# The first routing of an attention and mixture-of-experts chain: where its ranks, late parts, exponentials and first transposes stand in the order

## The chip, the cores and the metric

The program runs on one core of one Trainium2 chip. The metric is the device time of one execution in microseconds (us), as the median of several runs; for the kernel before it is 500.62 us (three runs, 499.69 to 501.07).

## The reference

Three stages follow each other. A linear attention with a decaying state runs over two sequences of 768 tokens (8 heads of 48). Its output, as 1536 tokens of 384 numbers, goes through a mixture of 8 experts where each token takes one (with a capacity of 384), and the result through a second one where each token takes two of 8, with noise in its gate.

```
state = alpha[t, :, None] * state + k[t] (x) v[t];   y[t] = q[t] . state        # per head
x = y as (1536, 384)
logits = x @ w_gate;  e = argmax;  gate = softmax(logits)[e]                    # layer 1
out1[i] = gate[i] * (relu(x[i] @ w1[e]) @ w2[e])     if fewer than 384 tokens came to e before i
noisy = out1 @ w_gate2 + log1p(exp(out1 @ w_noise)) * noise                     # layer 2
top2 of noisy, softmax over the two;  out[i] = sum_k weight[i, k] * (relu(out1[i] @ w1'[e_k]) @ w2'[e_k])
```

## The kernel before

All engines run lists that are written out in program order (`manual_schedule`); each engine takes its own list strictly in order, and a tile framework adds the semaphore waits that the data and the reuse of buffers ask for. PSUM tiles come in three rings: `ph` (3), `py` (3) and `pm` (2).

**Attention.** The tokens are cut into 12 chunks of 128 (6 of each sequence). A letter string says what is issued for chunk i, and in what order: S is `scores` of chunk i+1 (PE transposes the keys and forms two score tiles, ACT copies all three out of PSUM, POOL masks the scores with `affine_select`, L299), T is `state`, L is `logits` of chunk i-1, M is `mix` (the output `y`, copied by ACT as `yT`, L346), D is one step of `decays` (scans and products on VectorE, called DVE here, that prepare keys and queries of the next pieces), W is one split of a first-expert weight into a rounded part (ACT, L523) and a rest (POOL or DVE, L524), and R is one step of the routing. Chunks 0 to 7 use `PATTERN`, chunks 8 to 11 `PATTERN2` (L50 to L52, quoted in the diff).

**Logits.** `r1_logits` (L360) multiplies `yT` with the identity and the gate weights into one `pm` tile. From it DVE sums the gate logits (`gates`, L368), and ACT copies the token rows to SBUF (L389). For the chunks 8 to 11 (`EARLY` = 8) there are also "late parts": a rounded copy of the rows (ACT, L377) and its rest (DVE, `low`, L381), both read from the PSUM tile, since these tokens do not go to the first expert by way of DRAM.

**Routing.** `route1` is a generator for a group of chunks (`GROUPS`, L38: chunks 0 to 2, 3 to 5, 6 and 7, 8 and 9, 10, 11; called groups 0 to 5 here). Its steps are: maximum of the logits; its index; one-hot `oh`; the ranks on PE (L416 to L420, running counts by matrix products with a triangle) together with the exponential on ACT (L422); sums, the product with the rank tile and the reciprocal; slots and counts (L436 to L441); the scatter of the rows to DRAM by indirect DMAs from POOL (L158). Group 2's last step also loads the first expert's early tokens back (L447).

**First expert's tokens.** `first_x` (L589) transposes the early tokens with PE (L595), adds the late tokens by products of late parts with a slot matrix (L602), and splits the sum (ACT L609, DVE L610).

**Experts.** Sixteen jobs (8 experts, two layers) follow. `hidden` (L615) forms one block of 128 hidden units out of nine products, with weights and tokens each split in two parts (L623); `second` (L632) is the second product (L650). `split_x` (L570) transposes and splits the next job's tokens.

## Time and profile before

| what | value |
|---|---|
| median of three runs | 500.62 us (499.69 to 501.07) |
| the profiled execution | 503.19 us, of which the span of the trace is 501.4 us |
| PE (TensorE products) busy | 478.2 us, 95% of the span |
| DVE / ACT / POOL busy | 310.1 / 262.0 / 316.5 us |
| attention and first routing | until 98.51 us, when the first `hidden` starts |

The page gives the busy time of each engine, the span in 40 slices, the chain of work that ended last, and the costliest groups of instructions. PEclk is the TensorE clock granted in a stretch, as a share of 2.4 GHz. Times in the text are us from the start of the span.

### The profile page before, as it was taken

The page shows a single profiled execution, that of the slowest core. Times are in us where ns is not written, and L with a number is a line of the kernel's source. Part 1 is how long each engine was busy: PE and PEld are TensorE (multiplying, and loading weights), DVE is VectorE, ACT ScalarE, POOL GpSimd, SP SyncE. Part 2 cuts the span into 40 slices and gives each one's busy share as a digit, 9 for nine tenths or more (in the row PEclk, how much of TensorE's full clock was granted, in tenths as well). Part 3 has the DMA queues.
Part 4 walks back from the last instruction along what each step waited for, and adds up shares of the span by engine and source line. Part 5 has one row for each costly group of instructions (what it writes and reads, how often), then busy time and mean ns, then how long its engine had stood idle before and what let it go on. Part 6 is the DMA issues. An engine that isn't in the chain of part 4 may idle for free.

```text
span 501.4 us, 9823 instructions
## 1 busy us (share of the span) xinstructions
PE 478.2 (95%) x3539; PEld 448.2 (89%) x3542; DVE 310.1 (62%) x866; ACT 262.0 (52%) x682; POOL 316.5 (63%) x396
## 2 busy tenths in 40 slices
PE   8997999899999999999999799999999999999993
PEld 4586887799999999999988699899999999999993
DVE  8999956656786786776863323925545373655540
ACT  3475686366675676675661248353554535364410
POOL 3444674374876786785864149697594958779322
PEclk9999998999999999999999899999999999999997
DMA  8974663497888777676734644393564927372132
GB/s 287 406 246 160 242 221 127 164 295 233 282 288 249 261 241 241 202 244 203 239 100 130 204 92 132 99 245 106 156 176 129 221 81 203 83 191 25 17 47 43
DMA packets 47798, 91.67 MB, mean 183 GB/s; under 512 B 4624, under 2 KB 29153, under 8 KB 47738
## 3 DMA queue, kind: packets, MB, share of 16 engines
q1 hardware_dynamic: 38090, 70.32, 42.9%
q0 software_dynamic: 9648, 20.61, 17.4%
q8 instruction: 30, 0.49, 0.4%
q14 instruction: 30, 0.25, 0.2%
HBM read 70.63 MB, written 20.28 MB: 181 GB/s over the span
## 4 chain that ended last, share of the span: by engine, by line
PE 73%; DVE 14%; issue 4%; ACT 4%; DMA 2%; POOL 1%; SPq 0%; POOLq 0%; DVEq 0%; ACTq 0%
PE py L650 28%; PE ph L623 27%; DVE s L524 2%; PE pm L582 2%; PE ph L290 2%; DVE h L627 2%; PE pm L366 2%; DVE s L237 2%; PE pm L834 1%; PE py L337 1%; PE pm L678 1%; PE py L343 1%; PE ph L861 1%; ACT s L523 1%; PE py L317 1%
## 5 line engine op out<-in xcount | busy, mean ns | idle before, releaser
L524 POOL TENSOR_TENSOR s<-s,s 128x384 fp32r<-128x384 f32 x175 | 184.8, 1301 | 51.0 <-ACT s L523 45.9
L623 PE MATMUL ph<-x,s 128*128 128x240 f32 (+6 forms) x1152 | 179.9, 311 | 3.1 <-DVE h L627 1.4
L623 PEld LDWEIGHTS ph<-x,s 128*128 128x128 f32 x1152 | 167.6, 189 | 6.9 <-DVE h L627 3.0
L650 PE MATMUL py<-h,s 128*128 128x240 f32 (+5 forms) x1008 | 154.1, 307 | 0.0
L650 PEld LDWEIGHTS py<-h,s 128*128 128x128 f32 x1008 | 142.5, 189 | 1.0
L523 ACT ACTIVATE s<-s 128x384 fp32r<-128x384 f32 x256 | 123.1, 516 | 0.0
L627 DVE SCALAR_TENSOR_TENSOR h<-ph,h 128x240 fp32r<-128x240 f32 (+6 forms) x128 | 61.0, 483 | 67.4 <-ACT h L626 62.0
L524 DVE TENSOR_TENSOR s<-s,s 128x384 fp32r<-128x384 f32 x81 | 89.8, 1128 | 5.6 <-ACT s L523 5.5
L626 ACT ACTIVATE h<-ph 128x240 fp32r<-128x240 f32 (+6 forms) x128 | 55.3, 432 | 62.8 <-PE ph L623 53.5
L158 POOL DMA_INDIRECT out<-b,m_ix x29 | 46.5, 1605 | 45.5 <-ACT b L802 21.0
L586 ACT ACTIVATE x<-pm 128x480 fp32r<-128x480 f32 (+7 forms) x38 | 18.5, 489 | 63.9 <-PE pm L582 63.5
L299 POOL TENSOR_SCALAR_AFFINE_SELECT h<-h 128x512 f32<-128x512 f32 x24 | 22.6, 964 | 39.2 <-ACT h L298 39.2
L158 POOL DMA_INDIRECT xs<-b,m_si x32 | 32.9, 1028 | 15.8 <-DVE pm L759 10.5
L587 DVE TENSOR_TENSOR x<-pm,x 128x480 fp32r<-128x480 f32 (+7 forms) x38 | 20.7, 550 | 31.8 <-ACT x L586 31.5
L650 PE MATMUL py<-s,h 128*128 128x384 f32 x144 | 26.6, 340 | 0.0
L650 PEld LDWEIGHTS py<-s,h 128*128 128x128 f32 x144 | 25.0, 188 | 0.0
L237 DVE TENSOR_TENSOR s<-s,s 112x256 f32<-112x256 f32 (+2 forms) x24 | 19.0, 813 | 0.8 <-DMA s<-qs 0.2
L158 POOL DMA_INDIRECT xs<-s,m_si x12 | 13.1, 1088 | 9.8 <-DVE m_g L405 4.6
L156 POOL MEMSET spacer<- 1x1 f32 x74 | 18.8, 253 | 0.1
L582 PE MATMUL pm<-iw,b 108*128 108x108 f32 (+5 forms) x129 | 18.5, 259 | 0.2 <-DVE accs L760 0.2
L170 PE MATMUL ph<-warm 128*128 128x512 bf16 x63 | 16.2, 410 | 1.7 <-POOL warm L165 1.5
L797 DVE TENSOR_REDUCE m_own<-m_ox 108x4 f32<-108x24 f32 (+1 forms) x6 | 1.1, 176 | 24.6 <-POOL m_ox L795 23.5
(234 smaller groups left out, 544.9 us busy)
## 6 DMA issues: line engine op xcount, KB each, us to landing
s<-w SPq DMA_DIRECT2D x64, 768.0 KB, 5.4
xs<-s SPq DMA_DIRECT2D x2, 1576.0 KB, 6.4
out<-s SPq DMA_DIRECT2D x4, 768.0 KB, 7.8
b<-xs POOLq DMA_DIRECT2D x4, 664.9 KB
b<-xs POOLq DMA_DIRECT2D x7, 369.4 KB
s<-as SPq DMA_DIRECT2D x2, 780.5 KB
s<-ks SPq DMA_DIRECT2D x2, 768.0 KB, 9.5
s<-qs SPq DMA_DIRECT2D x2, 768.0 KB
```

Of the source, the lines that this page charges most:

```text
L156: G.memset(spacer, 0.0)
L158: st = G.indirect_dma_start(out=dst, out_offset=bass.IndirectOffsetOnAxis(ap=ix, axis=0), in_=src, in_offset=None, **kw)
L237: eng.tensor_tensor(o, src[:, h].rearrange("r (s j) -> r s j", j=64), x[:, h].rearrange("r (s j) -> r s j", j=64), op=ALU.mult)
L299: G.affine_select(a_, a_, pattern=[[0, 4], [1, 128]], compare_op=ALU.is_ge, fill=0.0, base=0, channel_multiplier=-1)
L523: A.activation(hi[sl], t[sl], AF.Copy)
L524: rest.append(lambda: (eng or V).tensor_tensor(lo[sl], t[sl], hi[sl].bitcast(F32), op=ALU.subtract))
L582: PE.transpose(xp[:, k * c + sl.start:k * c + sl.stop], g[:r, t, d * 128:(d + 1) * 128], ident[:r, :r])
L587: V.tensor_tensor(m(xl), xp[:, :w], m(xh).bitcast(F32), op=ALU.subtract)
L623: PE.matmul(p, w, x[:, d, :], start=(k == 0), stop=(k == 3 * ND - 1))
L626: A.activation(hh, p, AF.Relu)
L627: V.scalar_tensor_tensor(hl, p, 0.0, hh.bitcast(F32), op0=ALU.max, op1=ALU.subtract)
L650: PE.matmul(out_, l, r, start=(f == 0 and k == 0), stop=(f == NF - 1 and k == 2))
```

## The change

There are five edits.

- Each chunk has its own letter string (`PATTERNS`). The ranks of groups 0 and 1 now come two chunks behind their one-hots, right behind the scores of a later chunk. The weight splits start with three instead of five in chunk 7 and end in chunk 10 as before.
- In `route1` the exponential is a step of its own, ahead of the ranks. Groups take as many steps as before.
- In `r1_logits` the rows are copied out of PSUM first; a late part's rounded copy (ACT) and its rest (now on POOL) are made from that copy in SBUF. For groups of several chunks the gate sums follow the row copies, for single ones they stand ahead of them.
- At the end, `first_x`'s transposes and the ranks of group 4 stand ahead of the logits of chunk 11.
- `hidden` takes the three products with the tokens' low part last.

```
-FX = 4
-FXR = (3, 3, 0, 0)
+FXR = (4, 0, 1, 2)
-PATTERN = "WSDDWTWLRRRDDWMW"
-PATTERN2 = "WSRRRWTRWLRRRWMW"
-PLATE = 8
+PATTERNS = (
+    "SDDTDDM", "SDDTLDDM", "SDDTLDDM", "SDDTLRRRDDM", "SDDTLDDM", "SRRDDTLRRRDDM",
+    "SDDTLRRRDDM", "WSDDTWLDDMW", "WSRRWTRRRWLRRRWMW", "RWSRWTRRRWLWMW", "WSTWLRRRWMW", "RRRRLRRRRM")
...
-            if j >= EARLY:
+            if len(js) == 1:
                 gates()
             by = lambda x: x.rearrange("p (g a e) -> p g a e", g=4, a=2)
+            for ab in range(2):
+                A.activation(by(row[:, k, :DM])[:, :, ab, :], lv[:, :, ab * 64:ab * 64 + 48], AF.Copy)
+            if len(js) > 1:
+                gates()
             if j >= EARLY and first:
                 t = late[j] = sb([128, 2 * DM + C1], "b6", 5, F32R)
-                for ab in range(2):
-                    A.activation(by(t[:, :DM])[:, :, ab, :], lv[:, :, ab * 64:ab * 64 + 48], AF.Copy)
-
-                def low():
-                    for ab in range(2):
-                        V.tensor_tensor(by(t[:, DM:2 * DM])[:, :, ab, :], lv[:, :, ab * 64:ab * 64 + 48],
-                                        by(t[:, :DM].bitcast(F32))[:, :, ab, :], op=ALU.subtract)
-
-                if len(js) > 1:
-                    low()
-                else:
-                    lows.append(low)
-            for ab in range(2):
-                A.activation(by(row[:, k, :DM])[:, :, ab, :], lv[:, :, ab * 64:ab * 64 + 48], AF.Copy)
-            if j < EARLY:
-                gates()
+                A.activation(t[:, :DM], row[:, k, :DM], AF.Copy)
+                G.tensor_tensor(t[:, DM:2 * DM], row[:, k, :DM], t[:, :DM].bitcast(F32), op=ALU.subtract)
...
             V.tensor_tensor(oh, io8[:, None, :].to_broadcast(sh), i8[:, :n, 0:1].to_broadcast(sh), op=ALU.is_equal)
             yield
+            A.activation(ex, lm, AF.Exp)
+            yield
             rp = pm()
...
-            A.activation(ex, lm, AF.Exp)
-            while lows:
-                lows.pop(0)()
...
-                for (w, x) in ((wh, xh), (wh, xl), (wl, xh)):
-                    PE.matmul(p, w, x[:, d, :], start=(k == 0), stop=(k == 3 * ND - 1))
+                for (w, x) in ((wh, xh), (wl, xh)):
+                    PE.matmul(p, w, x[:, d, :], start=(k == 0), stop=False)
                     k += 1
+            for d in range(ND):
+                PE.matmul(p, w1_of(n, f, d)[0], xl[:, d, :], start=False, stop=(d == ND - 1))
...
-        while routes:
-            route_on()
-        logits(NCK - 1)
         fx = first_x()
-        for k in range(FX):
+        for k in FXR:
             next(fx)
-            for _ in range(FXR[k]):
+            for _ in range(k):
                 route_on()
+            if len(groups[-1]) and NCK - 1 not in grp:
+                logits(NCK - 1)
+                for _ in range(5):
+                    route_on()
```

How the order moves, at three places. Names: `pm_...`, `py_...` and `ph_...` are PSUM tiles, `m_oh_576` is the one-hot of group 0, `b_...` are early tokens or late parts.

PE in chunk 4, before: from the logits of chunk 3 to the start of the mix of chunk 4.

```order
L366 MATMUL pm_642<-s_4_80,h_599 128x120 x4
L416 LDWEIGHTS ones
L416 MATMUL pm_650<-eb_183,ones 128x24
L417 LDWEIGHTS ones
L417 MATMUL pm_650<-acc_187,ones 128x24
L419 LDWEIGHTS ones
L419 MATMUL pm_650<-m_oh_576,ones 128x16
L419 LDWEIGHTS ones
L419 MATMUL pm_650<-m_oh_576,ones 128x8
L420 LDWEIGHTS tri
L420 MATMUL pm_650<-m_oh_576,tri 128x24
L337 MATMUL py_666<-s_65_390,s_4_80 112x128 x4
```

PE in chunk 5, now: the same ranks, from the last score product of chunk 6 to the logits of chunk 4.

```order
L289 MATMUL ph_681<-s_81_472,s_80_471 128x128
L406 LDWEIGHTS ones
L406 MATMUL pm_697<-eb_183,ones 128x24
L407 LDWEIGHTS ones
L407 MATMUL pm_697<-acc_187,ones 128x24
L409 LDWEIGHTS ones
L409 MATMUL pm_697<-m_oh_576,ones 128x16
L409 LDWEIGHTS ones
L409 MATMUL pm_697<-m_oh_576,ones 128x8
L410 LDWEIGHTS tri
L410 MATMUL pm_697<-m_oh_576,tri 128x24
L365 MATMUL pm_712<-s_4_80,h_663 128x120 x4
```

The ranks left the place ahead of the mix of chunk 4; the mix of chunk 4 and the scores of chunk 6 now stand ahead of them.

ACT in chunks 9 and 10, before: from a weight split over the late part and the row of chunk 8 to `yT` of chunk 9 (L346).

```order
L523 ACTIVATE s_204_1077<-s_135_757 128x384
L377 ACTIVATE b_209_1089<-pm_1083 128x4x48 x2
L389 ACTIVATE s_206_1080<-pm_1083 128x4x48 x2
L523 ACTIVATE s_204_1077<-s_135_757 128x384
L346 ACTIVATE h_1111<-py_1098 112x512
```

The same stretch of ACT now (`yT` of chunk 9 is L345).

```order
L508 ACTIVATE s_192_1016<-s_168_906 128x384 x2
L374 ACTIVATE s_204_1074<-pm_1077 128x4x48 x2
L379 ACTIVATE b_207_1085<-s_204_1074 128x384
L508 ACTIVATE s_192_1016<-s_168_906 128x384
L345 ACTIVATE h_1103<-py_1090 112x512
```

The row copy came ahead of the late part, which now reads the row and not the PSUM tile.

PE at the end of the attention, before: from the last mix product over the ranks of group 4 to the first late part.

```order
L343 MATMUL py_1238<-h_1137,x_687 48x128
L416 LDWEIGHTS ones
L416 MATMUL pm_1254<-eb_183,ones 128x8
L417 LDWEIGHTS ones
L417 MATMUL pm_1254<-acc_187,ones 128x8
L420 LDWEIGHTS tri
L420 MATMUL pm_1254<-m_oh_1233,tri 128x8
L366 MATMUL pm_1276<-s_4_80,h_1251 128x120 x4
L595 MATMUL py_1287<-iw_83,b_203_1074 128x120 x4
L595 MATMUL py_1288<-iw_83,b_203_1074 128x120 x2
L602 MATMUL py_1287<-b_209_1089 128x240 x4
```

The same stretch of PE now.

```order
L342 MATMUL py_1235<-h_1131,x_671 48x128
L580 MATMUL py_1250<-iw_83,b_203_1070 128x120 x4
L580 MATMUL py_1251<-iw_83,b_203_1070 128x120 x2
L406 LDWEIGHTS ones
L406 MATMUL pm_1259<-eb_183,ones 128x8
L407 LDWEIGHTS ones
L407 MATMUL pm_1259<-acc_187,ones 128x8
L410 LDWEIGHTS tri
L410 MATMUL pm_1259<-m_oh_1229,tri 128x8
L365 MATMUL pm_1276<-s_4_80,h_1248 128x120 x4
L587 MATMUL py_1250<-b_207_1085 128x240 x4
```

The transposes of the early tokens (L595, now L580) moved from behind the logits of chunk 11 to ahead of the ranks and those logits.

## Rows read from the trace of the kernel before

**Rows 1.** The page: the clock granted to TensorE in 40 slices, in tenths.
```profile
PEclk9999998999999999999999899999999999999997
```

**Rows 2.** Busy time by stretch: us, then each engine's busy us, PEclk, DMA share.
```profile
48.00:53.00 5.00, 5.00 (x44) 4.15 (x43) 4.88 (x11) 1.14 (x2) 0.00 (x0) 0.66 0.96 342
...
83.00:87.00 4.00, 3.93 (x22) 3.68 (x24) 2.72 (x15) 3.29 (x10) 1.25 (x3) 0.57 0.58 169
```

**Rows 3.** Timeline of PE, chunks 4 to 8: start, us, work, [idle before <-releaser].
```profile
46.87 0.17 PE L416 MATMUL pm<-eb,ones 1*128 1x24 bf16 x1 [2.40 <-DVE m_l L368]
...
47.70 0.19 PE L419 MATMUL pm<-m_oh,ones 128*128 128x16 bf16 x2 [0.55 <-DVE m_oh L411]
...
47.78 1.11 PE L337 MATMUL py<-s,s 112*112 112x128 f32 x8
...
50.38 1.01 PE L284 MATMUL py<-iw,s 112*128 112x112 f32 x4
...
64.69 1.11 PE L337 MATMUL py<-s,s 112*112 112x128 f32 x8
...
66.74 0.60 PE L284 MATMUL py<-iw,s 112*128 112x112 f32 x4
...
68.36 0.54 PE L315 MATMUL py<-s,iw 48*64 48x192 f32 x4
```

**Rows 4.** Timeline of DVE in the same chunks.
```profile
43.82 2.51 DVE L237 TENSOR_TENSOR s<-s,s 112x768 f32<-112x768 f32 x2
...
47.47 0.18 DVE L411 TENSOR_TENSOR m_oh<-io,m_j 128x24 bf16<-128x24 f32 x1
...
48.86 0.17 DVE L240 COPY s<-s 112x12 f32<-112x12 f32 x1
...
53.38 0.96 DVE L237 TENSOR_TENSOR s<-s,s 112x768 f32<-112x768 f32 x1
...
59.28 2.26 DVE L237 TENSOR_TENSOR s<-s,s 112x768 f32<-112x768 f32 x2
```

**Rows 5.** Timeline of POOL in the same chunks: mask pairs, and the first scatter.
```profile
36.98 2.97 POOL L299 TENSOR_SCALAR_AFFINE_SELECT h<-h 128x512 f32<-128x512 f32 x2 [4.17 <-ACT h L298]
...
55.64 1.20 POOL L158 DMA_INDIRECT xs<-s,m_si  x1
...
60.03 2.00 POOL L299 TENSOR_SCALAR_AFFINE_SELECT h<-h 128x512 f32<-128x512 f32 x2
...
63.39 1.23 POOL L299 TENSOR_SCALAR_AFFINE_SELECT h<-h 128x512 f32<-128x512 f32 x2 [1.35 <-ACT h L298]
```

**Rows 6.** Timeline of ACT at the logits of chunk 8.
```profile
80.27 0.55 ACT L377 ACTIVATE b<-pm 128x192 fp32r<-128x192 f32 x2 [2.39 <-DVE m_l L368]
81.56 0.55 ACT L389 ACTIVATE s<-pm 128x192 f32<-128x192 f32 x2 [0.75 <-DVE b L381]
...
82.42 0.60 ACT L346 ACTIVATE h<-py 112x512 f32<-112x512 f32 x1
```

**Rows 7.** Timeline of PE, chunks 10 and 11 and the first expert's start.
```profile
83.07 1.85 PE L366 MATMUL pm<-s,h 112*128 112x120 f32 x8 [1.24 <-ACT h L346]
...
92.29 1.15 PE L366 MATMUL pm<-s,h 112*128 112x120 f32 x8 [0.52 <-DVE b L381]
93.28 1.50 PE L595 MATMUL py<-iw,b 120*128 120x120 f32 x12
94.54 0.92 PE L602 MATMUL py<-b 128*128 128x240 f32 x6
...
97.25 1.02 PE L602 MATMUL py<-b 128*128 128x240 f32 x6
98.51 1.67 PE L623 MATMUL ph<-x,s 128*128 128x240 f32 x5 [0.23 <-ACT x L609]
```

**Rows 8.** The DMA queue of SP: the load of the early tokens.
```profile
83.57 0.41 SPq L447 DMA_DIRECT2D b<-xs  x1
```

**Rows 9.** Timeline of PE in the tenth job.
```profile
323.25 1.25 PE L623 MATMUL ph<-x,s 128*128 128x432 f32 x5 [1.07 <-DVE x L587]
```

More of the change, by code (lines that the diff above doesn't have):

```diff
@@ L347, in mix @@
             yTs[i] = yT
-        scat1, grp, late, early, lows = [], {}, {}, [], []
+        scat1, grp, late, early = [], {}, {}, []
         def r1_group(js):
@@ L447, in route1 @@
                 nc.sync.dma_start(early[0], xs1[:C1].rearrange("(t p) d -> p t d", p=P1))
-            yield
         parts, raws, rest = {}, {}, []
@@ L988, in body @@
             left_ = int(DECAYS[i])
-            for o in PATTERN if i < PLATE else PATTERN2:
+            for o in PATTERNS[i]:
                 if o == "S" and si < NCK:
```

## The prediction, made before the change was run

> **What bounds the kernel now.** I read the page first. PE is busy for nearly the whole span, and its clock stands at full speed but for two slices with a digit 8 and the last one [rows 1], so the time is PE's own work plus the places where PE waits or runs slowly. The change touches the stage up to 98.51, where the first expert starts, and the order of products inside `hidden`. So next I read PE's timeline of that stage for its bracketed waits, then the windows for the clock behind them, then the timelines of the engines that PE waited for.
>
> Three places lose time. In chunk 4 PE has done the logits of chunk 3 and stands before the ranks of group 0: 2.40 us and then 0.55 us idle [rows 3]. DVE still works off the decays; the two last products of the piece run from 43.82 to 46.33, and the one-hot ends only at 47.65 [rows 4]. Behind this idle time PE's clock is 0.66 of full speed from 48 to 53, and only then full again [rows 2]. In chunk 10 PE waits 1.24 us for `yT` of chunk 9 [rows 7]; ACT came late to that copy, because it stood 2.39 us for a gate sum of DVE and 0.75 us for DVE's `low`, all three reading one PSUM tile in turns [rows 6]. From 83 to 87 the clock is 0.57 [rows 2]. Last, the logits of chunk 11 wait 0.52 us for DVE's `low`, which held a `pm` tile [rows 7].
>
> **Part 1, ranks two chunks later.** Nothing is added on any engine; the ranks go from ahead of the mix of chunk 4 to behind the scores of chunk 6. The stall goes with its slow stretch: 2.40 + 0.55 = 2.95 us idle, and 5.0 x (1 - 0.66) = 1.70 us of clock, together 4.65 us. What is late next? I replay PE from the rows. The logits of chunk 3 end at 46.87 - 2.40 = 44.5. A mix takes 66.74 - 64.69 = 2.05 us, a set of scores 68.36 - 66.74 = 1.62 us [rows 3]. So the scores of chunk 6 start at 46.5, and the keys and queries they read are ready at 46.33: just in time. They end at 48.1, the one-hot is there since 47.65, so the ranks don't wait. DVE's own list keeps its length: the later steps of group 0, which fill 47.65 to 48.86, move behind two steps of the next piece. That piece ends at 61.54 before [rows 4] and, as no work is added, at 61.5 or a little earlier now; the scores that read it started at 66.74 and should come at 66.74 - 4.65 = 62.1. It holds, by 0.6 us.
>
> POOL is tighter. Group 0's scatters wait for slots that DVE now makes behind those two decay steps. The steps ran on DVE from 48.86 to 54.34 [rows 4]; 1.2 us earlier they end at 53.1, a gate sum and the larger half of group 0's block follow (0.2 + 0.8 us), and I put the slots at 54.1 and the first scatter at 54.2, against 55.64 before. Scatters took from 55.64 to 60.03, and the mask pair behind them 2.00 us [rows 5]. So this pair, which belongs to the mix of chunk 7, is done at 54.2 + 4.4 + 2.0 = 60.6. PE's mix of chunk 7 began at 64.69 behind the ranks of group 1, which have now left this place (0.2 us, an estimate: five overlapping products of 0.17 to 0.19 us [rows 3]). Less that and 4.65, and with 1.1 us of products that need no mask [rows 3], it wants the mask at 60.9. Margin 0.3 us. If the pair takes 2.97 us, as the one at 36.98 did [rows 5], PE waits 0.7 us. I take 0.2 us for this, and 0.1 us for the logits of chunk 5, whose `pm` tile is freed by group 0's product on DVE at about the moment when PE wants it (bounds 0 and 0.5).
>
> The row shows mask pairs of 2.97 and 2.00 us beside DVE's two-input products and 1.23 us where DVE stood idle [rows 5]. The Trainium skill, "SBUF — State Buffer", section "SBUF: two separate sides", says that VectorE and GpSimd share one port pair as an exclusive lock: a GpSimd operation that reads SBUF and a VectorE operation with two SBUF inputs exclude each other for a whole instruction. By that rule the pair could wait out both products of 59.28, 1.23 + 2.26 = 3.5 us, PE would stand 1.2 us at the mix of chunk 7, and the sum below would be 1.0 us smaller; by the rows the pair overlapped these very products and took 2.00 us. I follow the rows.
>
> **Part 2, late parts from row copies.** ACT's two copies (0.55 us) of the row now follow the logits directly; the rounded copy is one of 128x384 where there were two of 128x192 (0.55 us in all [rows 6]), and I count it the same. DVE loses the `low` products; POOL gains four rests of 128x384. For one of those I use the nearest row, half a mask pair of 128x512: 0.6 to 1.5 us [rows 5], taking 1.0. ACT no longer stands 2.39 + 0.75 us. The copy of `yT` of chunk 9 ran from 82.42 to 83.02, and the logits followed at once [rows 6, 7]; ACT has to be 1.2 us earlier there and becomes about 3 us earlier; two more weight splits in chunk 10 come behind it or cost it up to 1 us. The wait goes, with its clock: 1.24 + 4.0 x (1 - 0.57) = 1.24 + 1.72 = 2.96 us.
>
> **Part 3, the end.** The 0.52 us at 92.29 goes, since the transposes (94.54 - 93.28 = 1.26 us [rows 7]) cover ACT's copy of the last `yT`, and `low` holds no PSUM tile. What is late next is the last late part: after the logits (0.99 us) come DVE's steps of group 4 (about as long as the 1.2 us of group 0's), a gate sum, two ACT copies in a row (1.1 us) and POOL's rest, 4.0 to 4.9 us from the logits' start. PE needed from 92.29 to 97.25, 4.96 us, of which the transposes now stand ahead: 3.7 us [rows 7], and its first product reads the rounded half only. So PE waits 0.2 to 1.1 us; as much of this follows copies that DVE and ACT may give earlier (both idle there), I take 0.2 and count 0.3 us of gain (bounds -0.6 and 0.5). The early tokens' load was issued at 83.57 and used at 93.28 [rows 7, 8]. It moves by about 4.65 us to 78.9 and its use by the whole gain to about 84; 5 us are left for the load. I charge 0.3 us (bounds 0 and 1.5).
>
> **Part 4, low products last in `hidden`.** The number of products and weight loads stays. In steady state `xl` is long there, so nothing. It can help where `xl` is late: 0.23 us at 98.51 [rows 7] and 1.07 us in the tenth job [rows 9], where five of nine products waited for DVE. Now six products go first, but the last `xl` is no earlier, and the three behind it still take their time. I take 0.3 us for both (bounds 0 and 1.3).
>
> **Exponential ahead of the ranks.** It runs on ACT behind score copies. Its cover is the stretch of scores between it and the sums on DVE; without it the sums would start about one small ACT step later, off PE's path. Nothing.
>
> **Sum.** 4.65 + 2.96 + 0.3 + 0.3 - 0.2 - 0.1 - 0.3 = 7.6 us. Against the profiled execution's own 503.19 us this gives 495.6. That execution stands 2.57 us above the median of the runs, so I take the difference off the median: 500.62 - 7.6 = 493.0 us. With all losses gone (2.95 + 1.70 + 2.96 + 0.52 + 1.3 = 9.4, and half a microsecond for what I can't see) it would be 490.7.
>
> **Rivals.**
> 1. *A new wait in the place of the old.* One of the near ties (mask of chunk 7, early tokens, last late part) turns into a stall of about 1 us, and the clock falls behind it as it did behind 1.24 us: 1.0 + 1.7 = 2.7 us, 495.7 us; two of them 498.4. For it: margins of 0.3 to 0.6 us. Against: PE waited 0.52 us at 92.29 and products behind it ran at their usual length.
> 2. *DVE becomes the bound of the first half.* If the decays keep the scores of chunk 9 back, most of Part 1 is lost there: 500.62 - (7.6 - 4.65) = 497.7 us. For it: DVE is nearly without gaps up to 61.5. Against: the scores started 5.2 us after it, more than the 4.65 won.
> 3. *Hidden anyway.* The first expert starts earlier but waits for weights that come at their old time: about 500.6. Against: PE's slices behind 100 us are full [rows 1], so weights were ahead of it.
> 4. *Slower: POOL binds from chunk 7 to 11.* Scatters, weight rests and four new rests stand in one list with the masks. If each mix waits for its masks by 0.8 us (about what the long pair costs) and the clock falls behind each wait by 1.7 us, a chunk costs 2.5 us; from the fourth such chunk (10 us against the 7.6) the change loses, and with five it is 500.62 - 7.6 + 12.5 = 505.5 us. Against: mask pairs without DVE work beside them took 1.23 us, and masks are made a chunk ahead of their use.
>
> **How the numbers follow.** Forecast 0.60, rival 1 0.20, rival 2 0.07, rival 3 0.06, rival 4 0.07. A difference under 0.3%, 1.5 us, can't be told from none here. Faster is the forecast with rivals 1 and 2, 0.87; the same 0.07; slower 0.06. The range runs from 490.7, all losses gone, to 498.0, which takes in rival 2 and rival 1 up to almost its second stall. The forecast's own range is 491 to 494.5.
>
> **What would show it.** In the new profile PE goes from the logits of chunk 3 to the mix of chunk 4 without a gap; the clock is full from 23 us to the end of the attention, both dips gone; ACT copies the row of chunk 8 without waiting for DVE; PE has no wait for `yT` in chunk 10; `hidden` starts near 91 us and the rest of the program takes what it took. It is wrong if PE's timeline shows a new bracket of 1 us or more, at the mix of chunk 7, at the transposes or at the last late part, or if `hidden` starts earlier but the expert stage grows by as much.

## The result, and the profile after

The changed kernel takes 495.13 us (median of four runs, 494.52 to 495.79) against 500.53 us before: 5.4 us faster, ratio 0.9894 [0.9872, 0.9916]. In a later comparison of the same two programs it was 497.68 against 503.3 us, ratio 0.9891 [0.9845, 0.9937]. The forecast of 493.0 had the sign and the range right, and was 2.1 us too low.

The profiled execution took 494.52 us with a span of 492.6 us. First the page's clock row, which answers to [rows 1]:

```profile
PEclk9999999999999999999999999999999999999997
```

Both slices with an 8 are gone. The two stretches of [rows 2] now, with the same columns (the clock is the third number from the end):

```profile
48.00:53.00 5.00, 5.00 (x64) 4.29 (x60) 4.96 (x5) 2.89 (x7) 2.58 (x3) 1.00 0.97 339
...
83.00:87.00 4.00, 4.00 (x44) 3.57 (x42) 1.89 (x16) 1.77 (x5) 1.85 (x3) 1.00 1.06 378
```

The clock is 1.00, the 2.4 GHz level, where it was 0.66 and 0.57 on average. The timeline of PE, from the first logits to the first hidden products, answers to [rows 3, 7]:

```profile
26.11 1.08 PE L365 MATMUL pm<-s,h 112*128 112x120 f32 x8
...
43.66 1.08 PE L365 MATMUL pm<-s,h 112*128 112x120 f32 x8
44.57 1.04 PE L336 MATMUL py<-s,s 112*112 112x128 f32 x8
...
48.41 1.13 PE L365 MATMUL pm<-s,h 112*128 112x120 f32 x8
...
54.33 1.12 PE L365 MATMUL pm<-s,h 112*128 112x120 f32 x8 [0.32 <-DVE m_se L412]
...
62.00 0.31 PE L342 MATMUL py<-h,x 128*48 128x128 f32 x1 [0.33 <-POOL h L298]
...
72.39 1.08 PE L365 MATMUL pm<-s,h 112*128 112x120 f32 x8
...
81.63 0.17 PE L409 MATMUL pm<-m_oh,ones 128*128 128x8 bf16 x1 [0.19 <-DVE m_oh L400]
81.91 1.15 PE L365 MATMUL pm<-s,h 112*128 112x120 f32 x8
...
91.62 0.49 PE L608 MATMUL ph<-x,s 128*128 128x240 f32 x2 [0.24 <-ACT x L594]
...
92.46 0.75 PE L608 MATMUL ph<-x,s 128*128 128x240 f32 x4 [0.35 <-ACT x L594]
```

The mix of chunk 4 (L336 at 44.57) follows the logits of chunk 3 at once, and the logits of chunk 9 (78.24) and of chunk 10 (81.91) do not wait for anything. The rows at 48.41 and 72.39 are the logits of chunks 4 and 8, which serve as marks below. What is left are four small waits: at the logits of chunk 5, at the masks of chunk 7, at the ranks of group 3 and at ACT's copies of the first tokens. The first `hidden` starts at 91.62, where it was 98.51 [rows 7].

In the text below, the *routing stretch* is the time from the first logits (26.11 here, 25.85 before) to the first hidden product. It leaves out the experts and most of the loading at the start. It is 91.62 - 26.11 = 65.5 us here; before it was 98.51 - 25.85 = 72.7 us. The time from the first logits to those of chunk 8 splits it: what Part 1 changes lies ahead of this mark, what Parts 2 and 3 change behind it. It is 72.39 - 26.11 = 46.3 us here. Before, with these rows for the logits of chunks 4 and 8, it was 75.82 - 25.85 = 50.0 us:

```profile
53.01 1.15 PE L366 MATMUL pm<-s,h 112*128 112x120 f32 x8
...
75.82 1.08 PE L366 MATMUL pm<-s,h 112*128 112x120 f32 x8
```

### The profile page after: what moved, and what is told of

It reads as the page before. It is cut to its first block, busy times and chain, and to the rows that moved or that the text cites. A ratio compares the mean times of both kernels' runs of the same rounds, so it can differ in the third digit from the quotient of the medians.

```text
span 492.6 us, 9810 instructions
## 1 busy us (share of the span) xinstructions
PE 475.3 (96%) x3539; PEld 445.4 (90%) x3542; DVE 317.3 (64%) x858; ACT 263.2 (53%) x678; POOL 320.7 (65%) x400
## 4 chain that ended last, share of the span: by engine, by line
PE 83%; DVE 7%; issue 3%; ACT 3%; POOL 3%; DMA 1%; POOLq 0%; DVEq 0%; ACTq 0%
PE py L637 32%; PE ph L608 19%; PE ph L611 9%; PE ph L169 3%; PE pm L567 3%; DVE s L509 2%; PE ph L289 2%; PE pm L365 2%; DVE h L614 2%; PE py L316 2%; PE py L342 2%; PE pm L821 1%; PE py L336 1%; PE ph L848 1%; PE py L283 1%
## 5 line engine op out<-in xcount | busy, mean ns | idle before, releaser
L608 PE MATMUL ph<-x,s 128*128 128x240 f32 (+6 forms) x768 | 136.1, 313 | 0.9 <-ACT x L594 0.6
L608 PEld LDWEIGHTS ph<-x,s 128*128 128x128 f32 x768 | 115.5, 189 | 3.3 <-DVE h L614 1.2
L509 DVE TENSOR_TENSOR s<-s,s 128x384 fp32r<-128x384 f32 x81 | 96.3, 1211 | 3.3 <-ACT s L508 3.1
L611 PE MATMUL ph<-x,s 128*128 128x240 f32 (+6 forms) x384 | 77.2, 309 | 0.3 <-DVE x L572 0.2
L611 PEld LDWEIGHTS ph<-x,s 128*128 128x128 f32 x384 | 61.2, 189 | 1.3 <-DVE x L572 0.9
L298 POOL TENSOR_SCALAR_AFFINE_SELECT h<-h 128x512 f32<-128x512 f32 x24 | 22.7, 968 | 27.4 <-ACT h L297 27.3
```

Source lines behind the costliest of these rows:

```text
L298: G.affine_select(a_, a_, pattern=[[0, 4], [1, 128]], compare_op=ALU.is_ge, fill=0.0, base=0, channel_multiplier=-1)
L509: rest.append(lambda: (eng or V).tensor_tensor(lo[sl], t[sl], hi[sl].bitcast(F32), op=ALU.subtract))
L608: PE.matmul(p, w, x[:, d, :], start=(k == 0), stop=False)
L611: PE.matmul(p, w1_of(n, f, d)[0], xl[:, d, :], start=False, stop=(d == ND - 1))
```

## The experiments

Two theories stood against each other. One is the prediction's: idle time and slow clock of both places are losses that add up, each gone with its part of the change. Its rival: the losses are coupled, since a TensorE that comes earlier only waits longer for VectorE. All kernels ran beside the kernel before; runs of different groups were on different chips, so ratios compare better than times.

| kernel | median us | ratio to before | first logits to chunk 8 | routing stretch |
|---|---|---|---|---|
| first comparison: before | 500.53 | 1 | 49.97 | 72.7 |
| first comparison: after | 495.13 | 0.9894 [0.9872, 0.9916] | 46.28 | 65.5 |
| group 1: before again | 501.1 | 0.9980 [0.9952, 1.0007] | 51.04 | 71.4 |
| without Part 4 | 495.64 | 0.9872 [0.9831, 0.9912] | 46.90 | 66.1 |
| without Part 1 | 498.71 | 0.9939 [0.9911, 0.9967] | 50.83 | 70.1 |
| without Part 2 | 498.09 | 0.9919 [0.9885, 0.9953] | 46.29 | 68.8 |
| group 2: without Part 1, stall filled | 501.08 | 0.9952 [0.9929, 0.9976] | 49.52 | 69.7 |
| scatter behind masks | 498.86 | 0.9888 [0.9849, 0.9927] | 46.89 | 67.1 |
| middle third apart | 495.54 | 0.9849 [0.9810, 0.9888] | 46.30 | 65.3 |
| without Part 3 | 498.14 | 0.9891 [0.9853, 0.9930] | 46.31 | 66.3 |
| group 3: after again | 497.68 | 0.9891 [0.9845, 0.9937] | 46.63 | 65.9 |
| without Parts 1 and 2 | 503.56 | 1.0001 [0.9976, 1.0026] | 49.97 | 74.1 |
| tenth job's split | 496.69 | 0.9860 [0.9829, 0.9892] | 46.28 | 65.5 |
| thirds and split | 497.09 | 0.9858 [0.9825, 0.9892] | 46.55 | 65.6 |

The kernel before took 501.1 us in group 1, 503.66 in group 2 and 503.3 in group 3. The medians have their noise: the six runs of the kernel without Part 4 go from 494.27 to 499.08 us, so a difference of 3 us between two kernels of this table is not clear of it where their intervals touch. The last two columns are from one profiled execution each, in us. In three of these (without Part 4, after again, thirds and split) the clock was low right at the first chunk, 0.81 to 0.90 from 20 to 28 us against 1.00 in the first profile after, and the second logits came 7.7, 6.8 and 6.7 us behind the first instead of 5.85; their columns hold that.

### The kernel before, again

No edit.

> The kernel before, run again for a second profile, nothing changed. My sum (7.6 us) is larger than the gain between the medians (5.4 us) and smaller than that between the two profiled executions (8.7 us). Theory: each wait and each slow stretch that I counted belongs to the program, so a second profile shows the same two stretches at a clock near 0.6 (about 48 to 53 and 83 to 87) and a first hidden product near 98.5 us. Rival: the waits belong to the program, but how long the clock stays low behind them differs from execution to execution; then a second profile keeps the idle times of 2.9 and 1.2 us, shows a slow stretch missing or shorter, and starts the first expert 1.5 to 3 us earlier, near 96 to 97 us. Time ratio to the kernel before 1.000 under both.

Its windows at the two places, PE from the logits of chunk 8 on, and ScalarE's copy of `yT` of chunk 9:

```profile
48.00:53.00 5.00, 4.98 (x33) 4.12 (x32) 4.81 (x13) 0.69 (x2) 0.00 (x0) 0.50 0.97 346
...
83.00:87.00 4.00, 3.44 (x37) 2.94 (x36) 2.77 (x15) 3.31 (x11) 1.25 (x3) 1.00 0.35 83
```
```profile
77.21 1.08 PE L366 MATMUL pm<-s,h 112*128 112x120 f32 x8
...
83.17 1.15 PE L366 MATMUL pm<-s,h 112*128 112x120 f32 x8
...
87.19 0.17 PE L419 MATMUL pm<-m_oh,ones 128*128 128x8 bf16 x1 [0.75 <-DVE m_oh L411]
87.56 1.15 PE L366 MATMUL pm<-s,h 112*128 112x120 f32 x8 [0.18 <-ACT h L346]
...
97.59 0.38 PE L623 MATMUL ph<-x,s 128*128 128x240 f32 x1 [0.23 <-ACT x L609]
```
```profile
82.52 0.60 ACT L346 ACTIVATE h<-py 112x512 f32<-112x512 f32 x1
```

The same program in another execution: the slow stretch of chunk 4 is longer (0.50 on average against 0.66 [rows 2]), the second slow stretch is not there at all, and the 1.24 us [rows 7] has become 0.75 + 0.18 us. The two differences hang together. ScalarE copies `yT` of chunk 9 at the same time in both, 82.42 [rows 6] and 82.52. PE reached the logits of chunk 8 at 75.82 in the first profile and had to wait for that copy; here the longer slow stretch and a later start bring it there at 77.21, 1.4 us later, and its next logits (83.17) find the copy done. So a longer first loss took the second wait away, and no slow stretch followed. The routing stretch is 71.4 us, 1.2 shorter, and the execution took 500.58 us, close to the median, where the one that the prediction was worked out from took 503.19.

### Without Part 4

```diff
-                for (w, x) in ((wh, xh), (wl, xh)):
+                for (w, x) in ((wh, xh), (wh, xl), (wl, xh)):
...
-            for d in range(ND):
-                PE.matmul(p, w1_of(n, f, d)[0], xl[:, d, :], start=False, stop=(d == ND - 1))
```

> The changed kernel with the old order of products in hidden, nothing else undone. Theory (Part 4): 0.3 us slower than the changed kernel, with bounds 0 and 1.3: 495.4 us, and a wait for the low part back at the first expert and in the tenth job. Rival: the expert stage of the changed profile is 1.9 us shorter than before because of this order; then 496.5 to 497 us. Second rival: the 1.07 us of the tenth job came from a stall of DVE in one execution only; then no difference.

495.64 us against 495.13, with a ratio that is no larger than that of the kernel after: no effect that the runs can tell. In the tenth job the wait is there as before, 1.24 us for VectorE; in the two profiles of the kernel after it is 0.23 and 0.31 us, but another of 0.41 us, for the copy at L811, has come behind it. About half of that wait went, and a part of it was moved.

### Without Part 1

```diff
-"SDDTLRRRDDM", "SDDTLDDM", "SRRDDTLRRRDDM", "SDDTLRRRDDM", "WSDDTWLDDMW", "WSRRWTRRRWLRRRWMW"
+"SDDTLRRRDDM", "SDDTLRRRDDM", "SDDTLRRDDM", "SDDTLRRRDDM", "WSDDTWLRRRDDMW", "WSRRWTWLRRRWMW"
```

> The changed kernel with the ranks of groups 0 and 1 back behind the logits of chunks 3 and 6, all else as changed. Theory (Part 1): the stall of chunk 4 (2.95 us) comes back with 1.7 us of slow clock, and the new waits at the logits of chunk 5 and the mix of chunk 7 (about 1.2 us together) go: 3.4 us slower than the changed kernel, 498.5 us. Rival (the slow clock is not part of a usual execution): 1.7 us slower, 496.9 us, with the idle time there but full clock behind it.

498.71 us, and both waits are back in their place:

```profile
47.11 0.17 PE L406 MATMUL pm<-eb,ones 1*128 1x24 bf16 x1 [2.39 <-DVE m_l L367]
...
47.95 0.20 PE L409 MATMUL pm<-m_oh,ones 128*128 128x16 bf16 x2 [0.53 <-DVE m_oh L400]
...
54.13 1.15 PE L365 MATMUL pm<-s,h 112*128 112x120 f32 x8
```

The slow clock is there too:

```profile
48.00:53.00 5.00, 5.00 (x33) 4.14 (x34) 4.88 (x8) 0.62 (x3) 0.00 (x0) 0.50 0.96 339
```

Against the kernel without Part 4 (495.64), it is 3.1 us slower in the median, but the two ratio intervals touch, so the medians leave anything from nothing to more than 4.65 us open. The traces are sharper: the logits of chunk 8 come 50.83 us behind the first, in the kernel after 46.28, and at the first hidden product the difference is the same 4.5 us. The stall is Part 1's, with its slow clock, and its size is near the prediction's 4.65 less 0.3 us for new waits.

### Without Part 2

```diff
-                A.activation(t[:, :DM], row[:, k, :DM], AF.Copy)
-                G.tensor_tensor(t[:, DM:2 * DM], row[:, k, :DM], t[:, :DM].bitcast(F32), op=ALU.subtract)
+                for ab in range(2):
+                    A.activation(by(t[:, :DM])[:, :, ab, :], lv[:, :, ab * 64:ab * 64 + 48], AF.Copy)
...
+                        V.tensor_tensor(by(t[:, DM:2 * DM])[:, :, ab, :], lv[:, :, ab * 64:ab * 64 + 48],
```

> The changed kernel with the late parts made from the PSUM tile again (rounded copies on ACT, rests on DVE, gate sums ahead), all else as changed. Theory (Part 2): the wait for yT before the logits of chunk 9 comes back with a slow stretch, 2.5 to 3 us slower than the changed kernel, near 498 us. Rival: with the splits of the first weights spread otherwise ACT is early enough, and only the wait at the logits of chunk 11 comes back: 0.5 us, 495.6 us.

498.09 us, 2.5 over 495.64. The wait came back at two neighbouring places, with a slow clock (0.64) from 83 to 87 us:

```profile
82.70 0.17 PE L421 MATMUL pm<-m_oh,ones 128*128 128x8 bf16 x1 [1.15 <-DVE m_oh L410]
83.49 1.52 PE L365 MATMUL pm<-s,h 112*128 112x120 f32 x8 [0.59 <-ACT h L345]
```

The engines that make the late part wait for one another in that stretch, VectorE for ScalarE's rounded copy and ScalarE's row copy for VectorE's `low`:

```profile
81.33 0.62 DVE L380 TENSOR_TENSOR b<-pm,b 128x192 fp32r<-128x192 f32 x2 [0.62 <-ACT b L376]
```
```profile
81.99 0.55 ACT L388 ACTIVATE s<-pm 128x192 f32<-128x192 f32 x2 [0.69 <-DVE b L380]
```

The one-hot, and `yT` (L345), stand behind these turns on one PSUM tile. This run puts back the tile, the engine of the rest and the place of the gate sums together; which of the three costs most is not separated. The difference of 2.5 us between the medians is within overlapping intervals. In the traces it is 68.8 - 65.5 = 3.3 us, in an execution 2.2 us above its median.

### The stall of chunk 4, filled

The kernel without Part 1, with idle multiplications where PE waits:

```diff
             rk = rp[:, :n * E].rearrange("p (n e) -> p n e", e=E)
+            fill = first and js[0] == 0
+            if fill:
+                warm(11)
...
+            if fill:
+                warm(2)
             for k in range(n - 1):
```

> The kernel after with the ranks of groups 0 and 1 early again, as in the experiment on the ranks (498.7 us), but with idle multiplications of the constant tile put into the two waits of chunk 4: 11 of 128x512 ahead of the ranks of group 0 and 2 behind the first two rank products. The waits themselves stay (2.39 + 0.53 us in that experiment's profile), only TensorE is no longer idle in them. Theory (the clock falls because TensorE waits): the granted clock of 48:53, which was 0.50 there, stays near 1.0, and the 2.5 us that it took from five microseconds at half rate come back in part: 496.2 to 497.0, and what is left over the kernel after (495.1) is the idle part of the step. Rival (the low clock has another cause than this wait, or VectorE, busy 4.88 of these 5.00 us, would set the pace there anyway): 498.3 to 499.1, no change.

The clock followed the theory, the time the rival. First the window, then PE's timeline:

```profile
48.00:53.00 5.00, 4.89 (x57) 4.20 (x56) 4.88 (x11) 2.19 (x5) 0.24 (x1) 1.00 1.00 343
```
```profile
44.83 2.54 PE L169 MATMUL ph<-warm 128*128 128x512 bf16 x11
...
51.99 1.15 PE L365 MATMUL pm<-s,h 112*128 112x120 f32 x8
...
64.68 0.19 PE L414 MATMUL pm<-m_oh,ones 128*128 128x16 bf16 x2 [0.94 <-DVE m_oh L400]
...
86.29 0.17 PE L414 MATMUL pm<-m_oh,ones 128*128 128x8 bf16 x1 [1.36 <-DVE m_oh L400]
```

With PE busy in the stall, the clock stayed at 1.00 where it had been 0.50. The logits of chunk 4 start 2.4 us earlier, counted from the first logits: 51.99 - 26.37 = 25.6 us against 54.13 - 26.10 = 28.0 us. But two waits for VectorE's one-hots appear that the unfilled kernel does not have, 0.94 us at group 1 and 1.36 us at group 3. At the first hidden product 0.4 us is left (69.7 against 70.1), and the ratio, 0.9952, is no better than 0.9939. So the slow clock of chunk 4 comes from the idle PE, and in this kernel a full clock brings almost nothing, because VectorE is behind: it has no idle time from 51.56 us to the one-hot of group 1, which ends at 64.63. This does not size the clock term of Part 1, though. The wait of 0.94 us is at ranks that this kernel leaves early and Part 1 moves; in the kernel after they come behind the scores of a later chunk, at 64.63, and find the one-hot done since 64.29.

Why VectorE came late to the second one-hot stands in its own timeline and in GpSimd's:

```profile
80.45 3.24 DVE L514 TENSOR_TENSOR s<-s,s 128x384 fp32r<-128x384 f32 x1 [0.34 <-ACT s L513]
```
```profile
81.11 1.00 POOL L380 TENSOR_TENSOR b<-s,b 128x384 fp32r<-128x384 f32 x1
82.06 1.22 POOL L298 TENSOR_SCALAR_AFFINE_SELECT h<-h 128x512 f32<-128x512 f32 x2
```

A weight difference that takes 0.55 us elsewhere on VectorE took 3.24 us and was over at 83.69, 0.4 us after GpSimd's rest of a late part and its masks (83.28). The one-hot stood behind it. At 0.55 us it would have been over at 81.00, ahead of the rest; what held it until then is not shown.

### The scatter of group 0 behind the masks

```diff
-"SRRDDTLRRRDDM", "SDDTLRRRDDM"
+"SRRDDTLRRDDM", "SRDDTLRRRDDM"
```

> The kernel after with the scatter of group 0 one chunk later in the order, behind the masks of chunk 7 on GpSimd: the first indirect transfers, started at 55.72 us in the profile after, no longer stand ahead of those masks (59.96), on which the products of chunk 7 waited. Theory (the later ranks put the scatter in the way of the masks; this is the term of 0.2 us that came out larger): the wait of 0.33 us at L342 goes and the mix of chunk 7 takes some 2.0 us instead of 2.74, 0.3 to 0.8 us faster than the kernel after: 494.3 to 494.8. Rival (the scatter, now behind the masks, delays the weight load that waits for it or the masks of chunk 8, which stood in a pair with those of chunk 7): no change or up to 0.5 us slower, 495.1 to 495.6.

Neither. The wait for the masks is gone, but the ranks of two groups now wait for one-hots, 1.19 us at group 1 and 1.37 us at group 3. Those of group 1 on PE, their one-hot on VectorE, and GpSimd beside it:

```profile
65.93 0.19 PE L409 MATMUL pm<-m_oh,ones 128*128 128x16 bf16 x2 [1.19 <-DVE m_oh L400]
```
```profile
64.85 1.03 DVE L400 TENSOR_TENSOR m_oh<-io,m_j 128x24 bf16<-128x24 f32 x1
```
```profile
63.90 1.94 POOL L509 TENSOR_TENSOR s<-s,s 128x384 fp32r<-128x384 f32 x2
```

The one-hot, 0.18 to 0.22 us elsewhere, took 1.03 us and ended with GpSimd's two weight differences (65.84), which stand at this place in the new order. The routing stretch grew by 1.5 us. In time the kernel can't be told from the one after (0.9888).

### The middle third apart

```diff
-            xa, xc = py(), py()
-            at = (xa[:, :C1], xa[:, C1:2 * C1], xc[:, :C1])
+            xa, xc, xm = py(), py(), ph()
+            at = (xa[:, :C1], xm[:, :C1], xc[:, :C1])
```

> The kernel after with a PSUM tile of its own for the middle third of the transposed first tokens, which shared one with the first third. In the profile after, the first expert's hidden products start at 91.62 and wait 0.24 and 0.35 us for ScalarE's copies, which take turns with VectorE's differences on the shared tile. Theory (the sharing sets these waits): with tiles apart ScalarE's three copies run on end, the second wait of 0.35 us goes, 0.3 to 0.6 us faster: 494.5 to 494.8. Rival (the two engines read different tiles at no less cost, or the products only wait for the low part instead): within 0.2 us of 495.1.

Six hidden products run on end where there were two waits:

```profile
90.94 1.01 PE L608 MATMUL ph<-x,s 128*128 128x240 f32 x6
...
92.23 0.83 PE L608 MATMUL ph<-x,s 128*128 128x240 f32 x6
```

The second block begins 66.6 us behind the first logits instead of 67.3, 0.7 us earlier, and ScalarE's three copies run on end, where it waited 0.47 us for VectorE's difference in the kernel after; so the shared tile was what made ScalarE late. The ratio 0.9849 lies below the 0.9894 and 0.9891 of the kernel after, but the intervals overlap: shown in the trace, not in the time.

### Without Part 3

```diff
-FXR = (4, 0, 1, 2)
+FX = 4
+FXR = (3, 3, 0, 0)
...
+        while routes:
+            route_on()
+        logits(NCK - 1)
```

> The kernel after with the end of the first routing as before: the remaining steps and the logits of the last chunk ahead of the transposes of the first tokens, and the late products spread as before. All else as after. Theory (Part 3: TensorE then waits for the exponentials and one-hot rows of the last groups, 0.52 us at one place of the profile before, with nothing put under it): 0.3 to 0.5 us slower than the kernel after, 495.4 to 495.6, and a wait of some 0.5 us between 84 and 92 us in its profile. Rival (this order costs nothing, the waits move to the first hidden products, which wait for ScalarE in the profile after anyway): 494.9 to 495.3.

Two waits are back, this one and one of 0.24 us at the late products (91.44), and the routing stretch is 0.8 us longer (66.3):

```profile
85.89 1.15 PE L366 MATMUL pm<-s,h 112*128 112x120 f32 x8 [0.46 <-ACT h L346]
```

In the time (ratio 0.9891) it does not show; the 0.3 to 0.5 us expected are less than these runs can tell.

### The kernel after, again

> The kernel after, unchanged, beside the three others of this call. Theory (the routing stage does the same in every execution; what differs is where the granted clock falls later): from the first logits (26.11 us in its first profile) to the first hidden product of the first expert (91.62) 65.5 us again, within 0.2. Rival (the first profile was a lucky one, as that of before was an unlucky one): 66 to 68 us in that stretch. Its median: 495 on a chip like the first; on one where the kernel before takes 503.7, near 498.

65.9 us in the routing stretch, 0.35 over the first profile, just between theory and rival; 0.95 us more than in the first profile went ahead of the second logits, where the clock was low. The kernel with the tenth job's split, which is the same up to there, has 65.5. Behind its first chunk the stretch repeats well in this kernel, while that of the kernel before was 72.7 and 71.4.

### Without Parts 1 and 2

The two edits above together.

> The kernel after with Parts 1 and 2 both undone (the ranks of groups 0 and 1 early, the late parts from PSUM), Parts 3 and 4 as after. Undone one at a time they cost 3.6 and 3.0 us of the median, and 4.5 and 3.3 us from the first logits to the first hidden product. Theory (the losses are coupled: what TensorE loses in chunk 4 it need not wait for at chunks 9 and 10): less than the sum, 4.5 to 5.5 us slower than the kernel after in the median, and 70 to 71.5 us in that stretch against 65.5. Rival (they add, as the prediction had it): 6.6 us slower in the median and 73.3 us in that stretch.

In the profiled execution the losses added, as the rival had it: 74.1 us, 8.5 over the kernel after, where each part alone undone made 4.5 and 3.3. Both slow stretches are there in one execution:

```profile
48.00:53.00 5.00, 4.11 (x35) 3.20 (x34) 4.87 (x22) 0.82 (x2) 0.00 (x0) 0.76 0.95 344
...
87.00:92.00 5.00, 3.86 (x18) 3.54 (x17) 3.63 (x25) 2.38 (x9) 1.19 (x3) 0.61 1.02 349
```

That execution, 506.5 us, was the longest of this kernel's twelve, 2.9 above their median. The median is 5.9 us above that of the kernel after. That lies between theory (up to 5.5) and rival (6.6), and the noise covers both; within group 1, Part 1 undone cost 3.1 and Part 2 undone 2.5 us, 5.6 together. So neither the trace nor the medians support my theory that the two parts cut into each other, though the kernel before does so between its two executions. And this kernel, which keeps Parts 3 and 4, can't be told from the kernel before (1.0001 [0.9976, 1.0026], so within 1.3 us).

### The tenth job's split, and both edits

```diff
             eng = [G if x == "G" else V for x in ENGS[layer - 1]]
+            if n == E + 1:
+                eng[11] = G
```

> The kernel after with one small change in the tenth job, which Part 4 also touched: the two differences of weights that VectorE makes there (10.52 us for two, where 0.54 is usual, while GpSimd makes 18 of them on end) go to GpSimd as well. Theory (VectorE is held until GpSimd's run of 18 ends, and what stands behind on VectorE, the differences of the next tokens, comes late for TensorE, which waits 0.2 to 0.6 us for them and 0.4 at the weights behind): the two waits in the tenth job go and no slow clock follows, 0.5 to 2 us faster than the kernel after of this call. Rival (TensorE then waits for GpSimd's longer run, 2 us more, or for ScalarE's copies instead): no change, within 0.3 us.

> The two that point ahead, together: the kernel after with the middle third apart and with the tenth job's two differences on GpSimd. Theory: the first brings 0.4 to 0.7 us (in its own run the products of the second hidden block began 0.74 us earlier, counted from the first logits), the second 0.5 to 2 us, so 1 to 2.5 us faster than the kernel after of this call. Rival (the first gain is lost again at the later waits): the same as the split alone, within 0.3 us.

The kernel after, GpSimd and VectorE in the tenth job, first GpSimd's whole run, which is of 21 differences and not of 18, then its last two and VectorE's two one by one:

```profile
292.04 21.34 POOL L509 TENSOR_TENSOR s<-s,s 128x384 fp32r<-128x384 f32 x21
```
```profile
310.53 1.54 POOL L509 TENSOR_TENSOR s<-s,s 128x384 fp32r<-128x384 f32 x1
312.03 1.35 POOL L509 TENSOR_TENSOR s<-s,s 128x384 fp32r<-128x384 f32 x1
```
```profile
303.27 9.23 DVE L509 TENSOR_TENSOR s<-s,s 128x384 fp32r<-128x384 f32 x1 [0.68 <-ACT s L508]
312.42 1.37 DVE L509 TENSOR_TENSOR s<-s,s 128x384 fp32r<-128x384 f32 x1
```

With the edit, the same on GpSimd, VectorE and PE:

```profile
293.13 22.92 POOL L509 TENSOR_TENSOR s<-s,s 128x384 fp32r<-128x384 f32 x23
```
```profile
312.58 0.61 DVE L572 TENSOR_TENSOR x<-pm,x 128x432 fp32r<-128x432 f32 x1 [1.55 <-ACT x L571]
313.10 3.37 DVE L509 TENSOR_TENSOR s<-s,s 128x384 fp32r<-128x384 f32 x1
```
```profile
317.05 0.43 PE L821 MATMUL pm<-iw,b 128*108 128x128 f32 x2 [1.41 <-DVE b L811]
```

The two waits of 0.31 and 0.41 us (in the kernel after of this group) became one of 1.41 us: the next difference on VectorE, 0.54 us elsewhere, is held for 3.37 us until GpSimd's longer run ends, and `b` (L811) stands behind it. So the gap was moved to a later place, and it grew. 496.69 and 497.09 us against 497.68, intervals overlapping; no version here is shown to be faster than the kernel after.

## Why the prediction was right, and where it was 2 us off

**What bound the kernel: right.** All three losses were real and went where the prediction put them: no gap between the logits of chunk 3 and the mix of chunk 4, a full clock to the end of the attention, no wait for `yT` in chunk 10, `hidden` at 91.62 ("near 91").

**Part 1: the loss right in mechanism and size, the new waits too small.** "The stall goes with its slow stretch: 2.95 us idle, and 1.70 us of clock, together 4.65 us" held in the traces. Behind the first logits, the logits of chunk 4 come at 27.16 us before, 28.24 in before again, 28.03 without Part 1, and at 22.30 in the kernel after: 4.9, 5.9 and 5.7 us won, more than the 2.95 us of idle time, so the clock counted beside it. Its size follows the length of the slow stretch: before again is 1.08 us behind the first profile at chunk 4 and still 1.07 at chunk 8 (51.04 against 49.97). The terms that were too small are the 0.2 and 0.1 us for what comes late next. From chunk 4 to chunk 8 the kernel after takes 24.0 us and the other three 22.8, so its waits at the logits of chunk 5 (0.32 us, for VectorE) and at the masks of chunk 7 (0.33 us, for GpSimd) cost 1.2 us with what hangs on them, not 0.3. The first of them is rival 2, VectorE as the bound, at a small size. In all Part 1 won 3.7, 4.8 and 4.5 us at chunk 8; 4.65 - 0.3 = 4.35 were forecast.

**Part 1, what comes late next.** The order of engines was right, the scatter's start was not. I put it at 54.2 us:

```profile
54.60 0.17 DVE L425 TENSOR_REDUCE m_si<-m_t 128x3 int32<-128x24 f32 x1
```
```profile
55.72 1.19 POOL L157 DMA_INDIRECT xs<-s,m_si  x1 [4.20 <-issue]
...
59.96 3.19 POOL L298 TENSOR_SCALAR_AFFINE_SELECT h<-h 128x512 f32<-128x512 f32 x4
```

The slots were 0.7 us later than I had them, and the scatter began another 0.95 us behind them. The masks of chunk 7 then came at about 62.0, and PE waited 0.33 us. The pair itself took some 2.0 us (59.96 to the product that it released at 62.00), beside VectorE's two products of 59.19, which took 2.26 us, and not the 3.5 us that waiting out both products would make. But the reading that the pair "overlapped these very products" was wrong. Taken one by one, the operations took turns: VectorE's first product was over at 60.15, the first mask at 60.65, the second product at 61.46 and the second mask at 61.95. The row of 2.00 us in [rows 5] is made the same way. The trace so agrees with the rule of the Trainium skill, "SBUF — State Buffer", section "SBUF: two separate sides", that one such operation of VectorE and one of GpSimd exclude each other for a whole instruction; only the price of 3.5 us did not follow, since a mask came between the two products. The same rule bears on VectorE too, which GpSimd held up behind the moved scatter and in the tenth job.

**Part 2: the term that most likely carried the error.** "The wait goes, with its clock: 1.24 + 1.72 = 2.96 us" was right for the execution that was profiled: from the logits of chunk 8 to the first hidden product it took 22.7 us against 19.2 in the kernel after, 3.5 us with Part 3. In before again it took 20.4, so Parts 2 and 3 together were worth 1.15 us there, with waits of 0.75 and 0.18 us and a full clock. The wait was not a fixed loss: ScalarE's copy ends at about the same time, and how long TensorE waits for it depends on how late TensorE is already. Without Part 2 a slow stretch is there (0.64), without Parts 1 and 2 too (0.61), both a chunk later than before, so whether an execution usually has one is not shown; the three profiled executions that have it are 2.2 to 2.9 us above the medians of their kernels, and before again is 0.5 below. The 2.5 us between the medians say little by themselves, as their intervals overlap. Of the four rests of late parts in the profile after, three took 0.99 to 1.00 us on GpSimd, as estimated (1.0), and one 0.86.

**Parts 3 and 4: 0.6 us forecast, too small to tell.** Part 3 shows in the trace, 0.8 us of the routing stretch. Part 4 took the wait in the tenth job from 1.24 to 0.23 or 0.31 us, and 0.41 us came at the next place. Alone they left the time where it was within 1.3 us (1.0001).

**From the profile to the median.** "I take the difference off the median" carried the error over. The forecast of 7.6 us was near for the two profiled executions (503.19 to 494.52, 8.7 us). Of these, 72.7 - 65.5 = 7.2 us lie in the routing stretch, for which the terms without Part 4 made 7.3; this agreement is in part luck, as Part 1 won 3.7 of its 4.35 us there and what lies behind chunk 8 brought 3.5 of 2.96. 402.89 - 400.98 = 1.9 us lie in the experts (span less the start of `hidden`), which the change hardly touches and which took 400.3 to 404.2 us in the other profiles of changed kernels, and 0.3 us went the other way at the start. But the execution before stood 2.6 us above its median, and I named those 2.57 us without asking which of the terms they were. Set against before again, an execution near the median, the stretch gains 71.4 - 65.5 = 5.9 us (4.76 ahead of chunk 8 and 1.15 behind it), or 5.6 with after again: that is near the 5.4 to 5.6 us between the medians.

**The rivals.** A new wait of 1 us with a slow clock did not come; new waits of 0.3 us came without one. Weights did not hide the gain, and GpSimd did not become the bound.

## What to carry to other kernels

Losses read from one execution need not be there together in the next. A wait for another engine is only as long as PE is early for it; here a slow stretch that lasted 1.1 us longer took a later wait of 1.24 us and its slow clock away. So take a second profile of the kernel before, and mark the terms that only one of them shows, before their sum is taken off a median. What a slow clock costs depends on what stands next: it was carried in full where PE met no new wait, and nearly lost where PE then waited for VectorE's one-hots. And work that is moved to GpSimd does not leave VectorE alone: look in its timeline for differences that last until GpSimd's run ends.

## What was not expected of the hardware

How long the clock stays low differs between executions. Behind the same stall of 2.39 to 2.40 and 0.53 to 0.55 us the clock of 48 to 53 us was 0.66, 0.50, 0.50 and 0.76 in four profiles. Taken us by us it is at one of its two levels but for the edges: 0.50 (1.2 GHz) from 50 to 52 us in the first profile of before and from 47 to 53 in before again. The 0.76, without Parts 1 and 2, is no shallower: that execution came 1.5 us later and has 0.50 from 51 to 54, past the end of the window, and it reaches the logits of chunk 4 27.16 us behind the first, as the first profile does. The second slow stretch came behind the waits of [rows 7], of the kernel without Part 2 and of that without Parts 1 and 2, but not behind those of before again.

An operation of VectorE that reads two operands in SBUF can be held for as long as GpSimd works through its own without a pause. In the tenth job GpSimd's 21 differences lasted 1.35 to 1.64 us each as the profile has them, and the first 20 started every 0.97 us, so each began before the last was over. VectorE's first difference waited from 303.27 to 312.50, 0.4 us after the 20th of these (312.07). The 21st began only at 312.03, hardly before the 20th was over, and VectorE's second difference was done at 313.79, 0.4 us after the end of the 21st (313.38). With the edit, a difference took 3.37 us and was over at 316.47, 0.4 us after a run of 23 (316.05). In that last run VectorE's difference out of PSUM took its usual 0.61 us. The one-hot of 1.03 us looks the same at a smaller scale, and so does the end of the 3.24 us of the filled stall. The rule of the Trainium skill weighed in the prediction ("SBUF — State Buffer", "SBUF: two separate sides") says that whichever of the two comes second is blocked fully. Here the trace agrees, with 0.54 us grown to 3.37. That VectorE got no turn among 20 operations goes beyond the rule, which speaks of one instruction; it got one at the first place where GpSimd's operations no longer overlapped.
